# Attention and two feed-forward layers on one core: an earlier cut of d_ff for tiles 0 and 1, and a planner that runs forward and backward

## The chip, the cores and the metric

The kernel runs on one core of a Trainium2 chip. Its engines work side by side: TensorE (PE, with its weight loads as PEld), VectorE (DVE), ScalarE (ACT), GpSimd (POOL) and SyncE (SP), whose queue issues every DMA here. The metric is the device time of one execution in microseconds (us), the median over runs; less is better. Before the change it is 654.42 us (three runs, 654.26 to 655.8).

## The reference

What is computed, with the heads folded back into rows between attention and the first layer:

```python
scores = q @ k.T / 8                       # batch 2, 8 heads, 768 positions, head size 64
keep = (pos_k < n_sink) | (0 <= pos_q - pos_k < window)      # n_sink 4, window 128
a = exp(where(keep, scores, -1e9) - max);  a = a / (sum(a) + 1e-9)
x = (a @ v)                                # 1536 rows x 512
h = x @ w1_in;  g = max(h, 0) + alpha * min(h, 0);  x = g @ w1_out      # d_ff 2048
h = x @ w2_in;  g = max(h, 0) + log1p(exp(-abs(h)));  out = g @ w2_out  # d_ff 2048
```

## The kernel before

The 1536 rows are four tiles of 384 (t = 0 to 3). Attention of a tile is six groups, G = 6t to 6t+5; a group is 128 queries of two head pairs. `front` computes a group's scores on TensorE (L470, 24 matmuls), reduces and masks them on DVE (L475, four of them), exponentiates on ACT (L478, four) and scales (L492, on DVE, ACT or POOL); `back` turns them (L504 and L505, eight transposes), copies them out of PSUM (L160 or L156, two of 128x512), multiplies by the values (L523, 24 matmuls), and leaves x as a rounded half and a rest (L164, `x<-bank,x`, on DVE).

Each layer cuts d_ff = 2048 into 16 slices c. One (t, c) is a place p in a list. `g1` multiplies x by the slice of the first weights (12 matmuls, L274), an activation follows (`act1`: ACT L290 and L291, DVE L292, then two halves g by L156/L158/L160 and L164; `act2` in layer 2: ACT L309, L310, L312 and DVE L307, L313, L314, L164), and the second product is `g2` (12 matmuls, L327, in layer 1) or `g2_out` (9 matmuls, L368, in layer 2). The `h` of successive places lies in banks 4 and 5 by turns. A weight slice comes as 64-bit numbers and has to be converted first (`convert`): one load (SP) and, of about 1000 columns each, DVE L248, L250, L252, an ACT or POOL step (L239/L241), DVE L255, an ACT or POOL copy (L156/L158), DVE L164 (`w<-temp,w`). A slice is usable by TensorE only behind this last subtraction. Slices 0 to 15 of layer 1 are converted once, in order.

The order of layer 1 before: tiles 0 and 1 with slices 0 to 7, tile 0's eight first; then both with slices 8 to 15; then tiles 2 and 3 in the same way. The sums of `g2` collect in banks 0 to 3 over a run of slices and are then kept or added in SBUF (`keep_y`, L339 and L344). The attention of tile 1 is spread between the first slices of tile 0 and uses one bank pair (6, 7) throughout, as every later tile does; tile 0 has four pairs.

What sets the order on every engine is `Planned.run`: it holds all operations with a cost by engine, what they read and write, and a due time from the table `slots` (L565). It walks once through time and gives each free engine the ready operation with the earliest due time; an operation with a choice of engines goes where it would end first. The operations are then emitted in the order of their planned starts, so each engine's queue is in that order, and an instruction whose operand is late holds up all behind it on its engine. At run time nothing is reordered.

Two constraints matter at the step from layer 1 to layer 2: `act2` of odd places writes into the part of `late` that holds tile 3's kept sum, so it waits until the four L344 of tile 3 have read it; and `g1` of place p+2 waits until L314 of place p has read its bank.

Of the kernel before, what the change touches and what calls it, by code (L numbers as in the profile page):

```python
# [8 lines left out]
F32 = mybir.dt.float32  # L9
# [38 lines left out]
class Planned:  # L48
# [6 lines left out]
    TO_PE, FROM_PE, BETWEEN, FROM_DMA = 0.23, 0.20, 0.15, 2.2  # L55

# [28 lines left out]
    def run(self):  # L85
        ops = self.ops
        left = [len(o[2]) for o in ops]
        after = [[] for _ in ops]
        for n, o in enumerate(ops):
            for b in o[2]:  # L90
                after[b].append(n)
        engines = ("SP", "PE", "ACT", "DVE", "POOL")
        free = dict.fromkeys(engines, 0.0)
        waiting = {e: [] for e in engines}
        ready = {e: [] for e in engines}
# [8 lines left out]

        for n in range(len(ops)):
            if not left[n]:
                offer(n)
        def queue(e, n):
            due = ops[n][3] + 30
            return 1.8 * sum(ops[m][1][e] for d, m in ready[e] if m not in start and m != n and d <= due and len(ops[m][1]) == 1)  # L110

        t, force = 0.0, False
        while len(start) < len(ops):
            for e in engines:
                while waiting[e] and waiting[e][0][0] <= t + 1e-9:
                    n = heapq.heappop(waiting[e])[1]
                    if n not in start:
                        heapq.heappush(ready[e], (ops[n][3], n))
            for e in engines:
# [3 lines left out]
                while ready[e]:  # L123
                    due, n = heapq.heappop(ready[e])
                    if n in start:
                        continue
                    cost = ops[n][1]
                    mine = t + cost[e]
                    if not force and any(max(free[o], at(n, o)) + c + queue(o, n) < mine + queue(e, n) - 1e-9 for o, c in cost.items() if o != e):
                        later.append((due, n))  # L130
                        continue
                    start[n], end[n], on[n] = t, mine, e
                    free[e] = mine
                    for m in after[n]:
# [6 lines left out]
            nxt = [free[e] for e in engines if free[e] > t + 1e-9]  # L141
            nxt += [waiting[e][0][0] for e in engines if waiting[e] and waiting[e][0][0] > t + 1e-9]
            if len(start) < len(ops):
                force = not nxt
                t = min(nxt, default=t)
        for n in sorted(start, key=lambda n: (start[n], n)):
            ops[n][0](self.nc, on[n])
# [19 lines left out]
class Memory:  # L167
# [4 lines left out]
    def __init__(self, tc, ctx):  # L172
# [6 lines left out]
        self.temp = temp = pool.tile([128, 3 * 1024], F32, name="temp")  # L179
# [7 lines left out]
        self.ring = [(late[:, n * RB:(n + 1) * RB], ("ring", n)) for n in range(3)]  # L187
# [12 lines left out]
        self.z = [temp[:, 2048 + n * 512:2560 + n * 512].bitcast(BF16) for n in range(2)]  # L200
# [13 lines left out]
class Ffn:  # L214
# [7 lines left out]
    def convert(self, l, c, n, due, load):  # L222
# [20 lines left out]
        def first(nc, e):  # L243
# [5 lines left out]
            {"DVE": 0.69}, [hi, lo], [kz], due)  # L249
# [150 lines left out]
class Window:  # L400
# [15 lines left out]
    def ring(self, G, c):  # L416

        if G == 0 or G >= 12:
            n = (2 * G + c) % 3 if G else c
# [4 lines left out]
    def load(self, G, c, due):  # L424
        t, b, j, _, hp = self.where(G)
        buf, k = self.ring(G, c)

        def go(nc, e):
            if 0 < G < 12 and c == 0:
                self.kept[15 - G % 6] = self.mem.slot(f"w{15 - G % 6}", [128, 2 * RB], F32)  # L430
            nc.sync.dma_start(out=buf(), in_=self.kqv[b, j, hp + c])

        keys = [k] + ([("kqv", 15 - G % 6, 1)] if 0 < G < 12 and c == 0 else [])
        if 12 <= G < 14:
            keys += self.mem.under[(2 * G + c) % 3]
# [8 lines left out]
    def front(self, G, d0, d1):  # L444
# [6 lines left out]
        for c in range(2):  # L451
            buf, kr = self.ring(G, c)

            def scores(nc, e, c=c, buf=buf):
                ring = buf()
# [15 lines left out]
            add(scores, {"PE": 0.52}, [kr], kb, d0)  # L471
# [362 lines left out]
```

## Time and profile before

| | us |
|---|---|
| median of 3 runs | 654.42 |
| the profiled execution | 653.59 |
| its span, first to last instruction | 651.8 |
| busy in the span: PE, PEld | 627.3, 575.2 |
| busy in the span: DVE, ACT, POOL | 481.1, 315.2, 81.6 |

The execution's time is 1.8 us over its span. A busy PE is not a PE at its peak: matmuls are pipelined and the end of one lies past the start of the next, so how fast PE works is read from the distance between starts. The page's 40 slices have DVE at 8 or 9 tenths in nearly all of the first nine and PE at 5 to 8 tenths in the first three. From 390 us to 640 us PE is busy without a break.

### The profile page before, as it was taken

Reading aid. Unit: us, or ns where it says so; the run is one execution under the profiler, and the core shown is the slowest. Engines: PE = TensorE matmul, PEld = TensorE weight load, DVE = VectorE, ACT = ScalarE, POOL = GpSimd, SP = SyncE. Lnnn points to the kernel's source line nnn. Section 1 sums busy time; section 2 is a strip of 40 time slices with the busy share of each in tenths; the row PEclk is TensorE's granted clock in tenths of the full one; section 3 lists DMA queues with packets and bytes.
Section 4 is the critical chain, followed back from the end, with each engine's and each line's share of the span. In section 5 each row is a group of like instructions: output and inputs, shape, how many; then the busy total and the mean of one; then the engine's idle time right before and its main releaser. Section 6 shows DMA issues by size and latency. Waiting matters only on the chain.

```text
span 651.8 us, 10937 instructions
## 1 busy us (share of the span) xinstructions
PE 627.3 (96%) x4224; PEld 575.2 (88%) x4224; DVE 481.1 (74%) x1064; ACT 315.2 (48%) x707; POOL 81.6 (13%) x103
## 2 busy tenths in 40 slices
PE   5888999999999999999999989999999999999995
PEld 4677889999999999999999989999999999999994
DVE  5899999884454654469887988886787777677674
ACT  3776766663334543435643645553443433333332
POOL 1445423430000100002310201000000000000000
PEclk9999999999999999999999989999999999999999
DMA  7999350111211112056105630000010000000001
GB/s 270 350 363 398 129 208 2 52 52 55 96 54 52 51 51 73 5 202 251 64 1 182 213 123 1 0 1 2 1 41 9 33 17 1 0 25 25 2 1 53
DMA packets 15035, 57.14 MB, mean 88 GB/s; under 512 B 1920, under 2 KB 4480, under 8 KB 14976
## 3 DMA queue, kind: packets, MB, share of 16 engines
q1 hardware_dynamic: 14976, 56.37, 24.1%
q8 instruction: 35, 0.57, 0.4%
q14 instruction: 24, 0.20, 0.1%
HBM read 53.22 MB, written 3.15 MB: 86 GB/s over the span
## 4 chain that ended last, share of the span: by engine, by line
PE 81%; DVE 11%; DMA 3%; POOL 2%; issue 1%; ACT 0%; SPq 0%; POOLq 0%; DVEq 0%
PE bank L274 36%; PE bank L368 20%; PE bank L327 17%; PE bank L470 3%; PE bank L523 2%; DVE w L164 1%; DVE temp L255 1%; PE bank L504 1%; DVE g L164 1%; DVE temp L252 1%; PE bank L505 1%; DVE temp L248 1%; DVE r L292 1%; DMA w<-w 1%; DMA w<-kqv 1%
## 5 line engine op out<-in xcount | busy, mean ns | idle before, releaser
L274 PE MATMUL bank<-x,w 128*128 128x384 f32 x1536 | 297.1, 339 | 4.0 <-DVE late L314 2.1
L274 PEld LDWEIGHTS bank<-x,w 128*128 128x128 f32 x1536 | 271.0, 189 | 12.9 <-DVE late L314 2.6
L327 PE MATMUL bank<-g,w 128*128 128x384 f32 x768 | 154.2, 341 | 2.2 <-ACT g L156 1.9
L368 PE MATMUL bank<-w,g 128*128 128x512 f32 x576 | 143.1, 393 | 0.0
L327 PEld LDWEIGHTS bank<-g,w 128*128 128x128 f32 x768 | 132.2, 188 | 6.8 <-ACT g L156 2.4
L368 PEld LDWEIGHTS bank<-w,g 128*128 128x128 f32 x576 | 107.2, 188 | 19.6
L309 ACT ACTIVATE late<-bank 128x384 f32<-128x384 f32 x64 | 31.3, 491 | 120.6 <-PE bank L274 120.6
L290 ACT ACTIVATE r<-bank 128x384 f32<-128x384 f32 x64 | 31.3, 490 | 76.5 <-PE bank L274 71.0
L292 DVE SCALAR_TENSOR_TENSOR r<-r,alpha,r 128x384 f32<-128x384 f32 x64 | 41.0, 640 | 27.2 <-ACT r L291 27.1
L307 DVE TENSOR_SCALAR late<-late 128x384 f32<-128x384 f32 x64 | 23.8, 373 | 45.1 <-ACT late L310 45.0
L312 ACT ACTIVATE late<-late 128x384 f32<-128x384 f32 x64 | 33.5, 525 | 24.8 <-DVE late L307 24.7
L478 ACT ACTIVATE late<-late,st 128x224 f32<-128x224 f32 x72 | 33.8, 471 | 22.0 <-DVE st L475 22.0
L164 DVE TENSOR_TENSOR w<-temp,w 128x1024 fp32r<-128x1024 f32 x32 | 38.8, 1219 | 5.1 <-ACT w L156 2.9
L492 POOL TENSOR_SCALAR late<-late,st 128x224 f32<-128x224 f32 x33 | 25.0, 768 | 130.6 <-DVE st L483 89.6
L164 DVE TENSOR_TENSOR g<-r,g 128x384 fp32r<-128x384 f32 x64 | 37.2, 581 | 5.3 <-POOL g L158 4.1
L255 DVE SCALAR_TENSOR_TENSOR temp<-w,temp 128x1024 int32<-128x1024 int32 x32 | 40.0, 1250 | 0.9 <-ACT temp L239 0.7
L164 DVE TENSOR_TENSOR g<-late,g 128x384 fp32r<-128x384 f32 x64 | 35.5, 557 | 5.3 <-POOL g L158 0.4
L475 DVE CUSTOM_DVE_ANT_0 late<-bank,mask 128x224 f32<-128x224 f32 x72 | 24.2, 386 | 19.9 <-PE bank L470 19.7
L164 DVE TENSOR_TENSOR late<-late 128x384 f32<-128x384 f32 x64 | 35.5, 556 | 1.8
L313 DVE SCALAR_TENSOR_TENSOR late<-late 128x384 f32<-128x384 f32 x64 | 35.5, 556 | 1.6
L314 DVE SCALAR_TENSOR_TENSOR late<-bank,late 128x384 f32<-128x384 f32 x64 | 35.5, 556 | 0.0
L310 ACT ACTIVATE late<-late 128x384 f32<-128x384 f32 x64 | 33.4, 524 | 1.7
(87 smaller groups left out, 591.4 us busy)
## 6 DMA issues: line engine op xcount, KB each, us to landing
w<-w SPq DMA_DIRECT2D x32, 1023.8 KB, 5.2
late<-kqv SPq DMA_DIRECT2D x26, 400.0 KB, 3.7
w<-kqv SPq DMA_DIRECT2D x22, 400.0 KB, 6.5
out<-late SPq DMA_DIRECT2D x18, 128.0 KB, 1.7
out<-early SPq DMA_DIRECT2D x2, 256.0 KB, 2.7
out<-early SPq DMA_DIRECT2D x2, 128.0 KB, 2.5
raw<-nsw SPq DMA_DIRECT2D x1, 2.0 KB, 3.1
alpha<-alpha SPq DMA_DIRECT2D x1, 8.0 KB, 4.1
```

Source lines behind the costliest of these rows:

```text
L164: engine(nc, e).tensor_tensor(out, a, b, ALU.subtract)
L255: add(lambda nc, e: nc.vector.scalar_tensor_tensor(b, raw[0].rearrange("p n w -> p (n w)").bitcast(I32)[:, 0:2048:2], 13, b, ALU.logical_s ...
L274: nc.tensor.matmul(out=h, lhsT=w[:, a, kk], rhs=xt[:, b, kk], start=(kk == 0 and n == 0), stop=(kk == 3 and n == 2))
L290: add(lambda nc, e: nc.scalar.activation(r, h, AF.Relu), {"ACT": 0.485}, [kh], [("r", 0)], due)
L292: add(lambda nc, e: nc.vector.scalar_tensor_tensor(n, n, mem.alpha[:, c:c + 1], r, ALU.mult, ALU.add), {"DVE": 0.61}, [("r", 0), ("alpha", ...
L310: add(lambda nc, e: nc.scalar.activation(u, u, AF.Exp, scale=-1.0), {"ACT": 0.53}, [], [ku], due)
L312: add(lambda nc, e: nc.scalar.activation(l, w, AF.Ln), {"ACT": 0.53}, [kw], [kl], due)
L313: add(lambda nc, e: nc.vector.scalar_tensor_tensor(u, w, 1.0, u, ALU.subtract, ALU.subtract), {"DVE": 0.57}, [kw], [ku], due)
L314: add(lambda nc, e: nc.vector.scalar_tensor_tensor(l, h, 0.0, l, ALU.max, ALU.add), {"DVE": 0.56}, [kh], [kl], due)
L327: nc.tensor.matmul(out=self.mem.bank[m][:, 0:TT], lhsT=w[:, a, m], rhs=g[:, b], start=(ends[0] and part == 0 and n == 0), stop=(ends[1] an ...
L368: nc.tensor.matmul(out=self.mem.bank[bk], lhsT=g[:, a, m * 128:(m + 1) * 128], rhs=w[:, b], start=(c == 0 and part == 0 and n == 0), stop= ...
L478: add(lambda nc, e, u=u: nc.scalar.activation(s[:, u], s[:, u], AF.Exp, bias=st[:, 0, u:u + 1], scale=-1.0, accum_out=st[:, 1, u:u + 1]), ...
```

## The change

Five edits.

1. The list of layer 1 is cut at slice 4 for tiles 0 and 1 (`cuts`): tile 0 with slices 0 to 3, tile 1 with 0 to 3, tile 0 with 4 to 15, tile 1 with 4 to 15. Tiles 2 and 3 stay cut at 8. `keep_y` and the first and last flags of `g2` follow the cut.
2. Groups 6 to 9 of tile 1 get the four bank pairs in turn (`place`), as tile 0 has; groups 10 and 11 stay on banks 6 and 7. Their due times are closer (`30 + 4 * r`).
3. Scores of a group are one operation of 24 matmuls, where they were two of 12, and its two loads are one operation.
4. The ring for the loads of groups 16 to 23 has a fourth buffer, `spare`, which also holds the second 16-bit scratch of `convert`.
5. `run` plans nine times. `forward` is the old walk with due times given; `backward` walks from the end over the engines that the forward plan chose, and gives each operation an urgency, the latest moment at which it may end. Eight times the urgencies of the last plan become the due times of the next. The plan that ends first by its own costs is emitted.

```diff
-    def run(self):
+    def forward(self, due):
 ...
-                        heapq.heappush(ready[e], (ops[n][3], n))
+                        heapq.heappush(ready[e], (due[n], n))
 ...
+    def backward(self, end, on):
+        left = [len(a) for a in self.after]
+        done = {}
+        for n in range(len(ops)):
+            if not left[n]:
+                waiting[on[n]].append((0.0, n))
 ...
+                    free[e] = done[n] = t + ops[n][1][e]
+                    for m in ops[n][2]:
+                        left[m] -= 1
+                        if not left[m]:
+                            wanted = max(done[k] + self.lag(on[m], on[k]) for k in self.after[m])
+                            heapq.heappush(waiting[on[m]], (wanted, m))
 ...
+        last = max(done.values())
+        return [last - done[n] for n in range(len(ops))]
+
+    def run(self):
 ...
+        plans = [self.forward([o[3] for o in self.ops])]
+        for _ in range(self.AGAIN):
+            plans.append(self.forward(self.backward(*plans[-1][2:])))
+        last, start, end, on = min(plans, key=lambda p: p[0])
 ...
-            n = (2 * G + c) % 3 if G else c
+            n = (2 * G + c) % (3 if G < 16 else 4) if G else c
 ...
-        n0 = (0, 2, 4, 6)[G % 4] if G < 6 else 6
+        n0 = (0, 2, 4, 6)[G % 4] if G < 10 else 6
 ...
-            add(scores, {"PE": 0.52}, [kr], kb, d0)
+        add(scores, {"PE": 1.02}, list(kr), kb, d0)
 ...
-    layer1 = [(t0 + t, c0 + c) for t0 in (0, 2) for c0 in (0, 8) for t in range(2) for c in range(8)]
+    cuts = ((0, 4, 16), (0, 8, 16))
+    layer1 = [(2 * n + t, c, a, b) for n in range(2) for a, b in zip(cuts[n], cuts[n][1:]) for t in range(2) for c in range(a, b)]
-    slots = 8 * [6.8] + 32 * [5.3] + 88 * [4.2]
+    slots = 4 * [8.0] + 4 * [5.0] + 32 * [5.3] + 88 * [4.2]
```

Where it moves instructions, first on PE in the opening. In the names, `x0` and `x1` are the inputs of tiles 0 and 1, `w0` to `w15` the weight slices, L274 is `g1` and L327 `g2`. Before, at tile 1's first product:

```order
L327 MATMUL bank3_64<-g0_153,w6_922 128x384 x2
L327 MATMUL bank0_61<-g0_153,w6_922 128x384
L327 MATMUL bank1_62<-g0_153,w6_922 128x384
L327 MATMUL bank2_63<-g0_153,w6_922 128x384
L327 MATMUL bank3_64<-g0_153,w6_922 128x384
L274 MATMUL bank5_66<-x0_150,w7_1024 128x384 x6
L274 MATMUL bank4_65<-x1_151,w0_456 128x384 x12
```

The same place of the changed program (L318 is `g1`, L371 `g2`):

```order
L371 MATMUL bank0_61<-g0_154,w3_850 128x384
L371 MATMUL bank3_64<-g0_154,w3_850 128x384
L318 MATMUL bank5_66<-x1_152,w1_618 128x384 x3
L371 MATMUL bank1_62<-g0_154,w3_850 128x384 x2
L318 MATMUL bank4_65<-x1_152,w0_507 128x384 x6
L371 MATMUL bank2_63<-g0_154,w3_850 128x384 x2
L371 MATMUL bank1_62<-g0_154,w3_850 128x384
L371 MATMUL bank2_63<-g0_154,w3_850 128x384
L318 MATMUL bank5_66<-x1_152,w1_618 128x384 x6
L318 MATMUL bank4_65<-x1_152,w2_747 128x384 x12
```

Tile 1's products stood behind eight slices of tile 0; now they stand behind four, and work of both tiles is interleaved in pieces of a quarter or half of a slice.

On DVE, up to the last subtraction of weight slice 14 of layer 1, before (`st` and `mask` belong to attention, `r1` and `g` to the activation, `x2` to tile 2):

```order
L250 TENSOR_SCALAR temp_73<-temp_73 128x1024
L252 TENSOR_TENSOR temp_73<-temp_73 128x1024
L292 SCALAR_TENSOR_TENSOR r1_70<-r1_70,alpha_74,r0_69 128x384
L255 SCALAR_TENSOR_TENSOR temp_73<-w14_796,temp_73 128x1024
L164 TENSOR_TENSOR x2_152<-bank6_67,x2_152 128x2x128
L164 TENSOR_TENSOR g0_153<-r1_70,g0_153 128x384
L255 SCALAR_TENSOR_TENSOR temp_73<-w15_832,temp_73 128x1024
L164 TENSOR_TENSOR w14_1517<-temp_73,w14_1517 128x1024
```

and of the changed program (L207 is that L164, L299 is L255, L336 is L292, L294 and L296 are L250 and L252):

```order
L336 SCALAR_TENSOR_TENSOR r1_70<-r1_70,alpha_75,r0_69 128x384
L299 SCALAR_TENSOR_TENSOR temp_73<-w14_1062,temp_73 128x1024
L294 TENSOR_SCALAR temp_73<-spare_74 128x1024
L207 TENSOR_TENSOR g1_155<-r1_70,g1_155 128x384
L296 TENSOR_TENSOR spare_74<-spare_74,temp_73 128x1024
L207 TENSOR_TENSOR w14_1582<-temp_73,w14_1582 128x1024
```

The subtraction of slice 14 stands at nearly the same place of DVE's list, with slice 15 one step less far, and what was done of the activations ahead of it is one place more.

Last, PE at the step from layer 1 to layer 2, where `x1` is layer 2's first input and L368 is `g2_out`. Before:

```order
L274 MATMUL bank5_66<-x1_151,w1_2964 128x384 x12
L327 MATMUL bank0_61<-g0_153,w15_1544 128x384 x2
L327 MATMUL bank1_62<-g0_153,w15_1544 128x384 x2
L327 MATMUL bank2_63<-g0_153,w15_1544 128x384 x2
L327 MATMUL bank3_64<-g0_153,w15_1544 128x384 x2
L327 MATMUL bank0_61<-g0_153,w15_1544 128x384
L327 MATMUL bank1_62<-g0_153,w15_1544 128x384
L327 MATMUL bank2_63<-g0_153,w15_1544 128x384
L327 MATMUL bank3_64<-g0_153,w15_1544 128x384
L274 MATMUL bank4_65<-x1_151,w2_3006 128x384 x12
L368 MATMUL bank0_61<-w0_2904,g0_153 128x512 x2
```

and of the changed program (L412 is `g2_out`):

```order
L318 MATMUL bank5_66<-x1_152,w1_2964 128x384 x3
L371 MATMUL bank1_62<-g0_154,w15_1628 128x384 x2
L371 MATMUL bank0_61<-g0_154,w15_1628 128x384
L371 MATMUL bank1_62<-g0_154,w15_1628 128x384
L371 MATMUL bank2_63<-g0_154,w15_1628 128x384 x3
L371 MATMUL bank3_64<-g0_154,w15_1628 128x384 x3
L318 MATMUL bank5_66<-x1_152,w1_2964 128x384 x9
L318 MATMUL bank4_65<-x1_152,w2_2982 128x384 x12
L412 MATMUL bank0_61<-w0_2890,g0_154 128x512 x2
```

Nine of the twelve products of slice 1 moved from ahead of the last `g2` of tile 3 to behind it.

## Rows read from the trace of the kernel before

**Rows 1.** Stretches: busy us of each engine (instructions), granted clock, DMA.
```profile
core 0: us, PE busy (x) PEld busy (x) DVE busy (x) ACT busy (x) POOL busy (x), PEclk, DMA share, GB/s
20.00:40.00 20.00, 16.44 (x245) 12.58 (x242) 17.41 (x54) 14.29 (x39) 8.72 (x14) 1.00 0.91 358
40.00:60.00 20.00, 18.15 (x193) 16.24 (x190) 19.02 (x45) 14.51 (x37) 12.12 (x12) 1.00 0.95 380
60.00:92.40 32.40, 30.86 (x285) 26.94 (x284) 31.61 (x68) 23.23 (x57) 10.00 (x10) 1.00 0.47 170
380.00:390.00 10.00, 7.86 (x31) 6.84 (x30) 8.60 (x16) 5.49 (x12) 1.09 (x1) 0.83 0.18 75
```

**Rows 2.** Timeline of PE, 63 to 71 us: start, duration, what, count.
```profile
63.65 0.27 PE L504 MATMUL bank<-ident,late 128*128 128x128 f32 x1
...
64.44 2.34 PE L274 MATMUL bank<-x,w 128*128 128x384 f32 x12
66.71 1.12 PE L523 MATMUL bank<-late,w 96*64 96x128 f32 x24
67.76 0.79 PE L274 MATMUL bank<-x,w 128*128 128x384 f32 x3
...
70.09 1.00 PE L470 MATMUL bank<-w 64*64 64x224 f32 x24
```

**Rows 3.** Chain of waits near 100 us: start, us, what.
```profile
100.89 2.08 PE bank L327 x12
```

**Rows 4.** Timeline of DVE: the last subtractions of weight slices 8 and 14.
```profile
91.36 1.22 DVE L164 TENSOR_TENSOR w<-temp,w 128x1024 fp32r<-128x1024 f32 x1
...
136.94 1.22 DVE L164 TENSOR_TENSOR w<-temp,w 128x1024 fp32r<-128x1024 f32 x1
```

**Rows 5.** Timeline of PE at the same time.
```profile
138.02 0.61 PE L470 MATMUL bank<-late 64*64 64x224 f32 x12
```

**Rows 6.** Groups of DVE: busy us, mean ns, then idle before and releasers.
```profile
L292 DVE SCALAR_TENSOR_TENSOR r<-r,alpha,r 128x384 f32<-128x384 f32 x64 | 41.0, 640 | 27.2 <-ACT r L291 27.1
L255 DVE SCALAR_TENSOR_TENSOR temp<-w,temp 128x1024 int32<-128x1024 int32 x32 | 40.0, 1250 | 0.9 <-ACT temp L239 0.7
...
L164 DVE TENSOR_TENSOR g<-r,g 128x384 fp32r<-128x384 f32 x64 | 37.2, 581 | 5.3 <-POOL g L158 4.1 <-ACT g L156 0.3
...
L475 DVE CUSTOM_DVE_ANT_0 late<-bank,mask 128x224 f32<-128x224 f32 x72 | 24.2, 386 | 19.9 <-PE bank L470 19.7
```

**Rows 7.** Groups of ACT: an exponential, a 128x512 copy, the accumulator.
```profile
L478 ACT ACTIVATE late<-late,st 128x224 f32<-128x224 f32 x72 | 33.8, 471 | 22.0 <-DVE st L475 22.0
...
L156 ACT ACTIVATE late<-bank 128x512 f32<-128x512 f32 x31 | 17.5, 596 | 16.5 <-PE bank L505 16.3
L478 ACT ACTIVATION_READ_ACCUMULATOR late<-late,st 128x1 f32 x72 | 13.5, 188 | 0.0
```

**Rows 8.** Timeline of ACT: second step of the activation of the third product.
```profile
55.43 0.48 ACT L291 ACTIVATE r<-bank 128x384 f32<-128x384 f32 x1
```

**Rows 9.** Timeline of PE near 150 us: a group's second half of scores.
```profile
150.60 1.75 PE L274 MATMUL bank<-x,w 128*128 128x384 f32 x9
152.27 0.61 PE L470 MATMUL bank<-late 64*64 64x224 f32 x12
152.82 0.79 PE L274 MATMUL bank<-x,w 128*128 128x384 f32 x3
```

**Rows 10.** Timeline of all engines, 375 to 388 us: the step between the layers.
```profile
375.37 2.24 PE L327 MATMUL bank<-g,w 128*128 128x384 f32 x12
...
378.20 1.48 DVE L344 TENSOR_TENSOR early<-bank,late 128x384 f32<-128x384 f32 x3
...
379.53 2.25 PE L368 MATMUL bank<-w,g 128*128 128x512 f32 x9
...
379.73 0.87 ACT L309 ACTIVATE late<-bank 128x384 f32<-128x384 f32 x2 [2.25 <-PE bank L274]
...
383.32 1.01 DVE L314 SCALAR_TENSOR_TENSOR late<-bank,late 128x384 f32<-128x384 f32 x2
383.92 3.91 PE L274 MATMUL bank<-x,w 128*128 128x384 f32 x12 [2.14 <-DVE late L314]
```

More of the change, by code (lines that the diff above doesn't have):

```diff
@@ L55 @@
     TO_PE, FROM_PE, BETWEEN, FROM_DMA = 0.23, 0.20, 0.15, 2.2
+    ENGINES, AGAIN = ("SP", "PE", "ACT", "DVE", "POOL"), 8
     def __init__(self, nc):
@@ L83, in lag @@
         return self.FROM_PE if a == "PE" else self.BETWEEN
-    def run(self):
+    def forward(self, due):
         ops = self.ops
         left = [len(o[2]) for o in ops]
[L88 to L95, printed above, removed]
+        free = dict.fromkeys(self.ENGINES, 0.0)
+        waiting = {e: [] for e in self.ENGINES}
+        ready = {e: [] for e in self.ENGINES}
         end, on, start = {}, {}, {}
@@ L103, in offer, with queue, elsewhere @@
                 heapq.heappush(waiting[e], (at(n, e), n))
+        def queue(e, n):
+            return 1.8 * sum(ops[m][1][e] for d, m in ready[e]
+                             if m not in start and m != n and d <= due[n] + 30 and len(ops[m][1]) == 1)
+        def elsewhere(n, e, t):
+            mine = t + ops[n][1][e] + queue(e, n) - 1e-9
+            return any(max(t, free[o], at(n, o)) + c + queue(o, n) < mine for o, c in ops[n][1].items() if o != e)
         for n in range(len(ops)):
@@ L107, in run @@
                 offer(n)
-        def queue(e, n):
-            due = ops[n][3] + 30
-            return 1.8 * sum(ops[m][1][e] for d, m in ready[e] if m not in start and m != n and d <= due and len(ops[m][1]) == 1)
         t, force = 0.0, False
         while len(start) < len(ops):
-            for e in engines:
+            for e in self.ENGINES:
                 while waiting[e] and waiting[e][0][0] <= t + 1e-9:
@@ L123, in run @@
                 while ready[e]:
-                    due, n = heapq.heappop(ready[e])
+                    d, n = heapq.heappop(ready[e])
                     if n in start:
                         continue
[L127 to L130, printed above, removed]
+                    if not force and elsewhere(n, e, t):
+                        later.append((d, n))
                         continue
-                    start[n], end[n], on[n] = t, mine, e
-                    free[e] = mine
-                    for m in after[n]:
+                    start[n], end[n], on[n] = t, t + ops[n][1][e], e
+                    free[e] = end[n]
+                    for m in self.after[n]:
                         left[m] -= 1
@@ L140, in run @@
                     heapq.heappush(ready[e], x)
-            nxt = [free[e] for e in engines if free[e] > t + 1e-9]
-            nxt += [waiting[e][0][0] for e in engines if waiting[e] and waiting[e][0][0] > t + 1e-9]
+            nxt = [free[e] for e in self.ENGINES if free[e] > t + 1e-9]
+            nxt += [waiting[e][0][0] for e in self.ENGINES if waiting[e] and waiting[e][0][0] > t + 1e-9]
             if len(start) < len(ops):
@@ L450, in front, with scores @@
         mask = mem.mask[:, min(j, 2)]
[L451 to L455, printed above, removed]
+        bufs, kr = zip(*(self.ring(G, c) for c in range(2)))
+        def scores(nc, e):
+            for c in range(2):
+                ring = bufs[c]()
                 for part in range(2):
@@ L738 @@
         first = Window(mem, InOrder(nc), kqv)
-        first.load(0, 0, 0)
-        first.load(0, 1, 0)
+        first.load(0, 0)
         nc.sync.dma_start(out=mem.alpha, in_=alpha)
```

70 lines of the change are left out of this document (44 added, 26 removed).

## The prediction

> **What bounds the kernel now.** I read first the busy time by stretches [rows 1]. From 20 to 92 us DVE has no room: 17.4 of 20 us, 19.0 of 20, 31.6 of 32.4, while PE is busy for 16.4, 18.2 and 30.9 of the same. The DMA engines stand at 0.91 and 0.95 up to 60 us, but there is no load among what TensorE waits for; it waits for conversions and copies, which are DVE's and ACT's. From 390 to 640 us PE is busy without a break.
>
> Busy time hides how much PE loses, so I read its timeline by starts. Twelve matmuls of a slice take 2.08 us [rows 3]; a group's transposes 0.79 (63.65 to 64.44), its values 1.05 (66.71 to 67.76), its scores 0.93 (the 1.00 less the overlap of 0.07 that the values show) [rows 2]. These are the prices of undisturbed work. The twelve `g1` matmuls between two pieces of attention take 2.27 instead of 2.08 (64.44 to 66.71) [rows 2], so an interruption costs about 0.2 us.
>
> Now a balance. Slice 14's last subtraction ends at 136.94 + 1.22 = 138.16 [rows 4]. PE is then at the last half of a group's scores [rows 5], with 17 `g1`, 15.7 `g2`, 14.5 scores, 14 transposes and 14 values done: 32.7 x 2.08 + 14.5 x 0.93 + 14 x 0.79 + 14 x 1.05 = 107.2 us of work. It has lost 31 us. The whole change is about how many of these 31 come back, since afterwards PE works nearly without gaps to the end, and what PE gains there the end gains too. PE's instructions are the same in number in both programs.
>
> **The change part by part.**
>
> *The opening.* DVE paces it, so I count DVE's list ahead of slice 14's last subtraction in both orders. Changed against before, it holds one L292 (0.64), one L164 of `g` (0.58) and four L475 (0.39 each) more, and less one L255 (1.25) [rows 6] and two 128x512 copies, which go to ACT (0.60 each by ACT's price [rows 7]); casts and small steps both ways cancel. 0.64 + 0.58 + 1.56 - 1.25 - 1.20 = 0.3 us more: the same list. So slice 14 comes again at about 138. But PE has more to do ahead of its first use: in the new order `g1` of slice 14 is the 19th product (14 of tile 0 and four of tile 1 stand ahead; before, the 23rd). Ahead of it stand 18 `g1`, 17 `g2`, 15 scores, 15 transposes and 14 values: 35 x 2.08 + 15 x 0.93 + 15 x 0.79 + 14 x 1.05 = 113.3 us. If DVE keeps its pace and PE is then waiting at slice 14, PE stands 113.3 - 107.2 = 6.1 us further at the same moment. That is the gain if all goes well; DVE could also idle less than before, because two tiles give PE and ACT something to do sooner, so I put the upper end at -8.
>
> Against it stands ACT. All of tile 1's attention now comes ahead of slice 3. Up to the second step of the third product ACT's list before is reached at 55.43 + 0.48 = 55.9 [rows 8]. The fourth product of tile 0 in the new order has twelve more exponentials ahead of it (0.471 + 0.188 = 0.66 each) and eight more 128x512 copies (0.60) [rows 7]: 7.9 + 4.8 = 12.7 us, and with small steps (one activation step pair of 0.97 [rows 8] and some copies of x, less one conversion step) 14.5. ACT was at work for about 0.89 of the time (42.4 us of listed work since 8 us), so these take 16 us: ACT reaches that step at about 72, where DVE's list alone would put it near 67. In the worst case the 5.5 us are never regained and the gain is about 0; if they are, because eleven more slices follow in which ACT has room (23.2 of 32.4 us [rows 1]), it is 6.1. Value: -4, which leaves ACT a third of the gain. Ends: -8 and 0.
>
> *Whole scores instead of halves.* After 92 us, scores of eleven of the twelve groups 12 to 23 were cut in two by other matmuls; in the new order none is. The cut costs: a half goes from 152.27 to 152.82, 0.55, so two are 1.10 against 0.93, and the nine matmuls in front take 1.67 (150.60 to 152.27) against 9 x 2.08 / 12 = 1.56 [rows 9]. That is 0.2 to 0.28 a group. The pieces of attention between products fall from 47 to 39; 8 x 0.25 = -2.0. Ends: 0 (if the free time goes to the next wait) and -3.5 (0.28 for eleven groups and a few bubbles behind the split).
>
> *The step between the layers.* Before, the last `g2` of tile 3 starts at 375.37 and ends near 377.3. The four L344 follow it, to 378.20 + 1.48 = 379.68; L309 of place 1 may only write then and starts at 379.73; its chain (L309 to L314) ends at 383.32 + 1.01 = 384.3 with the second half, and PE waits 2.14 us for the first [rows 10]. The chain from the last `g2` to L314 is some 6.6 us; what PE had in hand was `g1` of slice 2 (2.08) and a first `g2_out` (2.05), 4.1 us, before `g1` of slice 3 needs the bank. Now nine of twelve matmuls of slice 1's `g1` (1.56) stand behind the last `g2`, so 5.7 us are in hand against a chain of about 6.7: the wait falls by 1.1 to about 1.0.
>
> Behind the wait of before the twelve matmuls take 3.91 us, where those at 375.37 take 2.24 [rows 10]: 1.67 lost. The granted clock of these 10 us is 0.83 [rows 1], a mix of the full 2.4 GHz and its half, and the half follows directly on the 2.14 us wait. In the opening, PE waits about 10 to 20 per cent of 40 us in small pieces, with the granted clock at 1.00 [rows 1]; a wait of 1.0 us is of that sort, so I expect 1.00 here and the 1.67 saved. The Trainium skill says the same of cause and effect, in "TensorE: Matmul & The Clock Gate", Part 1: The HAM clock gate: the array's clock is gated to half when PE has been idle, and activity gives it back; by that rule alone a shorter gap that still falls badly would keep its half clock, and the step would bring 1.1 instead of 2.7. Value: -1.1 - 1.6 = -2.7, taken as -2.5. Ends: 0 (nine matmuls only shift the wait) and -3.1 (the wait vanishes wholly).
>
> *The rest.* Loads: a group's two become one operation with both DMAs, and a fourth buffer frees the ring; no load is among what PE waits for, so 0. From the last matmul to the end nothing moves in kind; 0. The plan sets each instruction as late as its own costs allow, so a step that takes longer on the chip than in the plan has less slack, on all engines at once. The trace of before shows no such plan; below, 0; above, 4: twenty waits of 0.2 us, what an interruption costs [rows 2]. Value: +1, a quarter, since PE's list is long and steady after 390 us.
>
> *Sum.* -4 - 2 - 2.5 + 1 = -7.5 on the profiled execution's 653.59: 646.1. The median of before is 0.83 above its profiled execution, so the median of after should be 646.1 + 0.83 = **647.0**.
>
> **The rivals.**
>
> *ACT becomes the bound of the opening.* For it: the 72 against 67 above. Against it: 0.89 is a rate under waits, not a limit, and some copies may go to POOL, busy for 8.7 of 20 us [rows 1]. If the whole 5.5 us stay, the opening gives 0.6 instead of 4: 650.4, say 651. Chance 0.18.
>
> *Half clock in the opening.* Now `g1` of slice 1 for tile 1 stands in PE's list ahead of attention pieces of group 7, and slices 0 and 1 end about 6.7 us of DVE work apart with 2.08 us of products between: a wait of up to 4.5 us, longer than the one after which the clock halved. For it: the row at 383.92 [rows 10]. Against it: the clock stayed at 1.00 through all of the opening before [rows 1]. It costs up to 1.67 us [rows 10]: 648.5. Chance 0.15.
>
> *The opening's gain is eaten up and the boundary wait stays.* Only the whole scores count, against the tight plan: -2 + 1 = -1, 653. Chance 0.08.
>
> *Slower: fresh slices.* Slices 4 to 15 now come in a row for tile 0 alone, each needed as soon as it is converted, where before eight products of tile 1 gave DVE time to get ahead. DVE's new list from slice 7 to slice 14 holds 44.7 us of work, counted as above. Before, from slice 8 (91.36 + 1.22 = 92.58) to slice 14 (138.16) it took 45.6 us for 38.3 of listed work [rows 4], 1.19 for 1. If waits on ACT and POOL raise this, slice 14 is late. The gain in all, 6.1 here and 4.5 for scores and step less the 1, is 9.6; it is used up when slice 14 comes at 138.2 + 9.6 = 147.8, that is from 1.19 + 9.6 / 44.7 = 1.40 for 1 on. At 1.47 it comes 2.9 us later still, and the time is 654.42 + 2.9, about 657. For it: PE cannot fill such waits, as tile 1's rest stands behind tile 0's slices. Against it: DVE is already at 0.98 in that stretch [rows 1]. Chance 0.09.
>
> *The change does not do what it says:* excluded; the changed order shows tile 1 behind four slices and the nine matmuls behind the last `g2`.
>
> **How the numbers follow.** Forecast 647.0 with 0.50; the rivals 0.18, 0.15, 0.08, 0.09. The likeliest has -4 +- 2, -2 +- 1, -2.5 +- 1 and +1 +- 1.5: about 643 to 650.5. Below it stand -8 - 3.5 - 3.1 = -14.6 at the extreme; I go to 640.5, near the middle between that (639.8 with the median) and the forecast's own end. Above, 653.5 takes in the rivals of ACT, of the clock and most of the third; the last and the tails are left out. A change of 0.3% (1.96 us) is about what a measurement of this kernel can tell from none: faster is under 652.46, slower over 656.4. Faster: 0.47 of the forecast's 0.50, 0.14 of the clock's 0.15, 0.14 of ACT's 0.18, 0.03 of the third's 0.08: 0.78. Slower: 0.07 of the last rival, 0.04 of the tails of ACT and the third: 0.11. Within: 0.11.
>
> **What would show it.** Opening: tile 1's first product on PE between 68 and 75 us, slice 14's last subtraction within 3 us of 138, and PE's loss at that moment near 25 where it was 31. If ACT shows no idle time from 10 to 65 us and DVE's waits end on ACT, the rival of ACT holds; a granted clock under 1.00 before 90 us is that of the clock; slice 14 later than 146 us is the slower one. Scores: each in one piece of about 1.00 us from 92 us on. Step: a wait of at most 1.2 us for L314 and a granted clock of 1.00 around 380 us; a longer wait with 0.83 makes that term wrong. If from 390 us to the end PE has gaps that sum to over 2 us, the tight plan costs more than I gave it.

## The result and the profile after

The changed kernel takes 640.03 us (median of four runs, 639.41 to 641.09) against 654.34 for the kernel before in the same runs; the ratio is 0.978, 95% interval 0.9767 to 0.9794. The change gave 14.3 us where 7.4 were forecast, and the time lies half a microsecond under the low end of the range, 640.5. The profiled execution took 641.09 us, the longest of the four, with a span of 639.1; between the two profiled executions the difference is 12.5 us, and the account below is of these.

The balance of the prediction (time passed less PE's work at undisturbed prices) can be taken at any moment from the starts of the matmuls. So many us PE had lost by then:

| | by 40 us | 92.4 | 143 | 366 | 390 | 620 |
|---|---|---|---|---|---|---|
| before | 21.0 | 29.0 | 31.0 | 40.6 | 44.5 | 45.8 |
| after | 16.9 | 21.0 | 23.8 | 29.6 | 31.6 | 33.0 |

So the opening up to 143 us gave 7.2 us, the attention between products from 143 to 366 us 3.8, the step between the layers 1.9, and the rest -0.1: 12.8 in all, which is the difference of the spans (12.7).

The stretches after, which answer to [rows 1] (columns as there):

```profile
20.00:40.00 20.00, 17.91 (x303) 14.25 (x300) 19.71 (x77) 18.32 (x61) 14.90 (x23) 1.00 0.98 368
40.00:60.00 20.00, 19.69 (x204) 17.14 (x202) 17.73 (x46) 14.77 (x43) 15.12 (x17) 1.00 0.85 350
60.00:92.40 32.40, 31.76 (x238) 30.54 (x236) 31.39 (x53) 20.76 (x41) 10.84 (x10) 1.00 0.60 233
366.00:380.00 14.00, 12.27 (x64) 10.97 (x63) 13.39 (x26) 8.53 (x16) 2.76 (x2) 1.00 0.29 112
```

All three engines that feed PE are fuller from 20 to 40 us than before (DVE 19.7, ACT 18.3, POOL 14.9), and PE with them. The granted clock is 1.00 in each stretch, at the step between the layers too, which now lies between 366 and 380 us.

Slice 14's last subtraction, from DVE's timeline [rows 4], and PE at that time [rows 5]:

```profile
135.21 1.93 DVE L207 TENSOR_TENSOR w<-temp,w 128x1024 fp32r<-128x1024 f32 x1 [0.28 <-ACT w L199]
```

```profile
134.65 2.53 PE L371 MATMUL bank<-g,w 128*128 128x384 f32 x13
137.02 0.68 PE L318 MATMUL bank<-x,w 128*128 128x384 f32 x3
137.63 1.12 PE L568 MATMUL bank<-late 96*64 96x128 f32 x24
```

Slice 14 is ready at 137.1 (forecast 138), and PE takes up its first product (137.02, three matmuls) just then. By 138 us PE has done 114.2 us of work; 113.3 were reckoned ahead of that product, 107.2 were done before.

A group's scores are one piece from 92 us on, here from PE's timeline near 107 us; they answer to [rows 9]:

```profile
106.33 0.51 PE L371 MATMUL bank<-g,w 128*128 128x384 f32 x2
106.77 1.00 PE L514 MATMUL bank<-late 64*64 64x224 f32 x24
107.70 2.70 PE L371 MATMUL bank<-g,w 128*128 128x384 f32 x14
```

106.77 to 107.70 is 0.93, the undisturbed price. Last the step between the layers on PE, against [rows 10]:

```profile
365.10 3.80 PE L318 MATMUL bank<-x,w 128*128 128x384 f32 x21
368.74 2.25 PE L412 MATMUL bank<-w,g 128*128 128x512 f32 x9
372.71 2.35 PE L318 MATMUL bank<-x,w 128*128 128x384 f32 x12 [1.73 <-DVE late L358]
374.90 1.08 PE L412 MATMUL bank<-w,g 128*128 128x512 f32 x4
```

The wait fell from 2.14 to 1.73 us only, but the matmuls behind it take 2.35 us instead of 3.91.

### The profile page after: what moved, and what is told of

Its sections match the earlier page's. It is cut to its first block, busy times and chain, and to the rows that moved or that the text cites. A ratio compares the mean times of both kernels' runs of the same rounds, so it can differ in the third digit from the quotient of the medians.

```text
span 639.1 us, 10922 instructions
## 1 busy us (share of the span) xinstructions
PE 619.0 (97%) x4224; PEld 574.1 (90%) x4224; DVE 479.0 (75%) x1061; ACT 313.9 (49%) x704; POOL 82.8 (13%) x109
## 4 chain that ended last, share of the span: by engine, by line
PE 86%; DVE 7%; POOL 3%; ACT 2%; issue 1%; DMA 0%; DVEq 0%; POOLq 0%; ACTq 0%
PE bank L318 39%; PE bank L412 20%; PE bank L371 18%; PE bank L568 3%; PE bank L514 2%; POOL late L537 2%; PE bank L549 1%; DVE temp L299 1%; PE bank L550 1%; DVE late L520 1%; DVE r L336 1%; DVE g L207 1%; POOL g L201 1%; DMA raw<-nsw 0%; DVE early L520 0%
## 5 line engine op out<-in xcount | busy, mean ns | idle before, releaser
L318 PE MATMUL bank<-x,w 128*128 128x384 f32 x1536 | 293.3, 337 | 1.7 <-DVE late L358 1.7
L318 PEld LDWEIGHTS bank<-x,w 128*128 128x128 f32 x1536 | 269.9, 188 | 8.4 <-DVE late L358 2.2
L371 PE MATMUL bank<-g,w 128*128 128x384 f32 x768 | 152.4, 339 | 0.3 <-DVE g L207 0.2
L412 PE MATMUL bank<-w,g 128*128 128x512 f32 x576 | 143.0, 393 | 0.0
L371 PEld LDWEIGHTS bank<-g,w 128*128 128x128 f32 x768 | 132.8, 188 | 2.7 <-DVE g L207 0.5
L412 PEld LDWEIGHTS bank<-w,g 128*128 128x128 f32 x576 | 107.2, 188 | 19.5
L334 ACT ACTIVATE r<-bank 128x384 f32<-128x384 f32 x64 | 31.4, 490 | 76.2 <-PE bank L318 71.6
L336 DVE SCALAR_TENSOR_TENSOR r<-r,alpha,r 128x384 f32<-128x384 f32 x64 | 42.3, 661 | 25.7 <-ACT r L335 25.5
L351 DVE TENSOR_SCALAR late<-late 128x384 f32<-128x384 f32 x64 | 23.3, 364 | 40.3 <-ACT late L354 40.3
L356 ACT ACTIVATE late<-late 128x384 f32<-128x384 f32 x64 | 33.5, 524 | 23.7 <-DVE late L351 23.6
L207 DVE TENSOR_TENSOR w<-temp,w 128x1024 fp32r<-128x1024 f32 x32 | 41.4, 1294 | 2.0 <-POOL w L201 1.0
L207 DVE TENSOR_TENSOR g<-late,g 128x384 fp32r<-128x384 f32 x64 | 35.5, 555 | 9.6 <-ACT g L199 4.0
L299 DVE SCALAR_TENSOR_TENSOR temp<-w,temp 128x1024 int32<-128x1024 int32 x32 | 41.3, 1297 | 0.9 <-ACT temp L283 0.8
L537 POOL TENSOR_SCALAR late<-late,st 128x224 f32<-128x224 f32 x34 | 26.3, 785 | 107.9 <-DVE st L528 65.9
L207 DVE TENSOR_TENSOR g<-r,g 128x384 fp32r<-128x384 f32 x64 | 35.9, 561 | 4.1 <-POOL g L201 3.2
L207 DVE TENSOR_TENSOR late<-late 128x384 f32<-128x384 f32 x64 | 35.6, 556 | 1.6
L335 ACT ACTIVATE r<-bank 128x384 f32<-128x384 f32 x64 | 31.1, 486 | 9.8 <-DVE g L207 9.8
L358 DVE SCALAR_TENSOR_TENSOR late<-bank,late 128x384 f32<-128x384 f32 x64 | 35.5, 555 | 0.5 <-ACT late L356 0.5
```

What stands on the lines that cost most here:

```text
L207: engine(nc, e).tensor_tensor(out, a, b, ALU.subtract)
L299: add(lambda nc, e: nc.vector.scalar_tensor_tensor(b, raw[0].rearrange("p n w -> p (n w)").bitcast(I32)[:, 0:2048:2], 13, b, ALU.logical_s ...
L318: nc.tensor.matmul(out=h, lhsT=w[:, a, kk], rhs=xt[:, b, kk], start=(kk == 0 and n == 0), stop=(kk == 3 and n == 2))
L336: add(lambda nc, e: nc.vector.scalar_tensor_tensor(n, n, mem.alpha[:, c:c + 1], r, ALU.mult, ALU.add), {"DVE": 0.61}, [("r", 0), ("alpha", ...
L356: add(lambda nc, e: nc.scalar.activation(l, w, AF.Ln), {"ACT": 0.53}, [kw], [kl], due)
L358: add(lambda nc, e: nc.vector.scalar_tensor_tensor(l, h, 0.0, l, ALU.max, ALU.add), {"DVE": 0.56}, [kh], [kl], due)
```

## The experiments

All were timed beside the kernel before, whose median was between 653.76 and 655.00 us. A ratio and its 95% interval are estimated from the single runs and need not equal the quotient of the medians. Lost time is PE's, reckoned as in the table above, and is that of the one profiled execution.

**One part of the prediction at a time, in the kernel before.** The plan's order is kept, and single instructions are moved in it. `before_whole` joins the halves of the scores of groups 12 to 23 on PE alone:

```diff
+        halves = [n for n, o in enumerate(ops) if o[0].__name__ == "scores"]
+        for one, two in zip(halves[24::2], halves[25::2]):
+            order.remove(one)
+            order.insert(order.index(two), one)
```

> The kernel before in its own order, but from group 12 on the first half of a group's scores is moved behind, next to the second; no other engine's order changes. The term of the prediction: twelve halves joined at 0.25 us, some 2 us less: 651.5 to 652.5. Theory of the trace after (3.7 us between 143 and 366 us come from whole scores): 650 to 651. Theory that the pieces go at nothing, since the later first half delays DVE: 654 to 655.

Measured 648.94, ratio 0.9932 (0.9908 to 0.9956). The loss from 143 to 366 us fell from 9.6 to 6.3: 3.3 us, or 0.37 for each of the nine groups whose scores stood there in two pieces before. The term is real and larger than the prediction put it. The median is 4.8 under that of before; the interval of the ratio reaches from 2.9 to 6.0 us.

`before_step` moves the nine matmuls:

```diff
+        at = max(order.index(n) for n in last)     # the last g2 of layer 1
+        for n in late:                             # three of four parts of g1, slice 1
+            order.remove(n)
+        order[at - len(late) + 1:at - len(late) + 1] = late
```

> The kernel before in its own order, but nine of the twelve matmuls of slice 1's first product in layer 2 are moved behind the last g2 of layer 1; no other engine's order changes. The term of the prediction: the wait for L314 falls from 2.14 by 1.1 us and the matmuls behind it stay at the full clock (2.2 instead of 3.9 us): 651.7. Rival (the chain behind the last g2 starts later by as much): 654 to 655, the wait at 2 us and the clock at 0.83 as before.

Measured 652.28, ratio 0.9982 (0.9970 to 0.9994). From its timeline:

```profile
376.68 3.80 PE L280 MATMUL bank<-x,w 128*128 128x384 f32 x21
380.32 2.25 PE L374 MATMUL bank<-w,g 128*128 128x512 f32 x9
384.06 2.35 PE L280 MATMUL bank<-x,w 128*128 128x384 f32 x12 [1.50 <-DVE late L320]
```

and from ACT's:

```profile
380.52 0.87 ACT L315 ACTIVATE late<-bank 128x384 f32<-128x384 f32 x2 [3.81 <-PE bank L280]
```

The wait fell by 0.6 and not 1.1; the clock stayed full. The nine matmuls that PE now has in hand are also what the chain begins with: L315 (L309 before) waits for slice 1's product and starts at 380.52, where it started at 379.73 [rows 10]. So a part of the expected rival is there too. The loss from 366 to 390 us fell from 3.9 to 1.8. The medians differ by 1.5, the ratio stands for 0.4 to 2.0. This profiled run had lost 0.9 more by 143 us than that of before, in an order that was not changed there.

**The parts of the change.** First each undone in the changed kernel; the plan is made anew each time. `plan_once` sets AGAIN to 0; `cut_at_8` restores the cut and its slots; `one_pair` has `G < 6` in `place`; `half_scores` gives the planner two operations of scores:

```diff
-    ENGINES, AGAIN = ("SP", "PE", "ACT", "DVE", "POOL"), 8
+    ENGINES, AGAIN = ("SP", "PE", "ACT", "DVE", "POOL"), 0      # plan_once
-    cuts = ((0, 4, 16), (0, 8, 16))
+    cuts = ((0, 8, 16), (0, 8, 16))                             # cut_at_8
-        n0 = (0, 2, 4, 6)[G % 4] if G < 10 else 6
+        n0 = (0, 2, 4, 6)[G % 4] if G < 6 else 6                # one_pair
-        add(scores, {"PE": 1.02}, list(kr), kb, d0)
+            add(scores, {"PE": 0.52}, [kr[c0]], kb, d0)         # half_scores, c0 = 0, 1
```

> The changed kernel (640.0 us), but planned once forward, without the eight repetitions; cut, bank pairs, whole scores and ring stay. Theory 1 (the cut makes the gain of the opening, whole scores that of the attention behind it, the planner little): 640 to 643, PE's lost time at 143 us stays near 24 us. Theory 2 (the urgencies found from the end make most of the gain): 647 or more, and the lost time at 143 us near 29.

> The changed kernel with tiles 0 and 1 cut at slice 8 again and the slots of before. Theory 1 (the cut makes the gain of the opening, since more of PE's work lies ahead of slice 14): 646 to 648, lost time at 143 us back to 29 to 31 us. Theory 2 (planner) and theory 3 (the four bank pairs): 640 to 642, lost time at 143 us near 25.

> The changed kernel with groups 6 to 9 on banks 6 and 7 again. Theory 1 (the cut): 641 to 642. Theory 3 (the four bank pairs let attention of tile 1 run ahead, which is the 4 us that PE had gained by 40 us): 644 or more, with lost time of 20 us or more at 40 us where the changed kernel has 16.9.

> The changed kernel with a group's scores as two operations of 12 matmuls for the planner, the loads still merged. Theory 1 (whole scores are what saved 3.7 us between 143 and 366 us): 642 to 644, and the halves are apart again from 92 us on. Theory 2 (the planner): 640 to 641, since the urgencies keep the halves of a group together.

And `planner_alone`: the kernel before with `forward`, `backward` and the new `run`, nothing else.

> The kernel before (654.4 us) with nothing but the new planner: cut at 8, one bank pair for tile 1, half scores, ring of three. Theory 1 (cut and bank pairs give the planner something to use, the planner alone little): 650 to 654, lost time at 143 us 28 to 31. Theory 2 (the urgencies do it alone): 646 or less, lost time at 143 us 26 or less.

| | median us | ratio to before | lost by 40 us | by 143 | 143 to 366 | 366 to 390 |
|---|---|---|---|---|---|---|
| after | 640.03 | 0.978 (0.9767 to 0.9794) | 16.9 | 23.8 | 5.8 | 2.0 |
| plan_once | 650.16 | 0.992 (0.9891 to 0.995) | 18.8 | 30.2 | 8.8 | 3.9 |
| one_pair | 648.59 | 0.9911 (0.9893 to 0.9928) | 21.1 | 30.9 | 6.0 | 2.5 |
| cut_at_8 | 646.11 | 0.9869 (0.9851 to 0.9886) | 17.8 | 29.1 | 6.8 | 2.4 |
| half_scores | 641.54 | 0.9813 (0.9788 to 0.9837) | 17.4 | 24.3 | 5.7 | 1.9 |
| planner_alone | 646.32 | 0.9902 (0.9876 to 0.9928) | 19.8 | 27.1 | 8.3 | 0.2 |

No theory holds by itself. Cut, bank pairs and repeated plan are each worth 6 to 10 us when they are taken out last, together far more than the whole change. The planner alone makes about half of the change: 7.4 us by the medians, 6.4 by the ratio. It takes 3.9 off the opening's loss, 1.3 off that up to 366 us, and 3.7 off the step, where the changed kernel itself loses 2.0. Cut and pairs pay only together. By 143 us 27.1 us are lost with the planner and neither of them (with half scores and three buffers); 30.9 with the cut alone, 29.1 with the pairs alone, and 23.8 with both. Both without the repetition come to 30.2, 0.8 under before.

Two limits. The profiles of `plan_once`, `cut_at_8` and `one_pair` hold 3.4 to 6.8 us of half clock between 32 and 45 us, those of after and `planner_alone` none from 20 us on; how much of their loss is the clock's was not separated. And the profiled run of `plan_once` took 651.97 us, near the upper end of its eight runs (645.89 to 652.16), so its row is a dear one.

Whole scores as an operation are worth 1.5 us by the medians, within the scatter of `half_scores` (639.83 to 643.59). Its eleven groups behind 92 us have their scores in one piece all the same. That is not the urgencies' doing in general: in `planner_alone` five of twelve groups are still cut. The fourth buffer and the closer due times were not tried by themselves.

**What paces the opening.** Four kernels in the changed kernel's own order. Ten instructions more on one engine:

```diff
+        more = [15.0 + 5 * k for k in range(10)]
+            if more and start[n] >= more[0] and on[n] == "ACT":      # "DVE" in more_dve
+                more.pop(0)
+                self.nc.scalar.activation(self.junk, self.junk, AF.Copy)
```

> The changed kernel in its own order, with ten more ACT instructions of some 0.45 us (128x320 copies that nobody reads), one every 5 us of the plan from 15 to 60 us. Theory that ACT bounds the opening: 4 us or more slower, 643.5 to 644.5. Theory that DVE paces it and ACT follows with room: under 1.5 us slower, 640 to 641.5, slice 14 still ready near 137 us.

> The changed kernel in its own order, with ten more DVE instructions of some 0.47 us (128x320 subtractions that nobody reads), one every 5 us of the plan from 15 to 60 us. Theory that DVE paces the opening and ACT only half: 4 us or more slower, 644 to 645, slice 14 at 141 us instead of 137. Theory that ACT and DVE share the pace, each hiding half of what the other is given: 2 to 3 us slower, 642 to 643, as with ten more ACT instructions (643.0).

and less work on one, which the output then leaves out:

```diff
+            w = 128 if 3 <= G < 12 and e == "ACT" else 512           # less_act
+            copy(nc, e, a[h][0][:, 0:w], bank[h][:, 0:w])
+        few = 256 if l == 0 and c < 4 else 1024                      # less_dve, columns of L299
```

> The changed kernel in its own order; ACT's 17 copies of turned weights of groups 3 to 11 take 128 of the 512 columns only (the output leaves the rest out): about 0.33 us less each, 5.5 in all. Theory that ACT and DVE set the pace by turns, so that an instruction on either costs 0.6 of its length: 3 us faster, 636.5 to 637.5, and slice 14 ready near 134.5. Theory that DVE alone paces and ACT only could not take more: 639 to 640. Theory that ACT bounds: 635.

> The changed kernel in its own order; L299 of slices 0 to 3 of layer 1 takes 256 of the 1024 columns only (the output leaves the low bits of these weights out): about 0.9 us less each, 3.7 in all. Theory that ACT and DVE set the pace by turns: 2 us faster, 637.5 to 638.5. Theory that DVE alone paces: 3.5 us faster, 636 to 637, slice 14 ready near 133.5. Theory that ACT bounds: 639.5 to 640.5.

| | median us | ratio to before | lost by 143 us | slice 14 ready |
|---|---|---|---|---|
| after | 640.03 | 0.978 | 23.8 | 137.1 |
| more_act | 642.96 | 0.9847 (0.9823 to 0.987) | 26.2 | 139.5 |
| more_dve | 643.06 | 0.9817 (0.9791 to 0.9842) | 27.3 | 140.6 |
| less_act | 639.85 | 0.9772 (0.9756 to 0.9789) | 24.1 | 137.5 |
| less_dve | 638.38 | 0.9749 (0.9731 to 0.9766) | 21.8 | 134.9 |

5.5 us less on ACT (17 copies, by their durations) bring nothing. Of 3.3 us less on DVE (four L299; 3.7 were reckoned) 2.0 come through by 143 us, and slice 14 comes 2.2 us sooner. Slice 14's last subtraction on DVE's timeline, of less_act and then of less_dve:

```profile
135.60 1.93 DVE L207 TENSOR_TENSOR w<-temp,w 128x1024 fp32r<-128x1024 f32 x1 [0.28 <-ACT w L199]
```

```profile
132.99 1.93 DVE L207 TENSOR_TENSOR w<-temp,w 128x1024 fp32r<-128x1024 f32 x1 [0.28 <-ACT w L199]
```

Only less and more together tell this: by more_act alone ACT would have seemed as much of a bound as DVE. How more_act costs its 2.4 us is seen on PE, on DVE, and in the stretch between (columns as in [rows 1]):

```profile
33.79 1.68 PE L573 MATMUL bank<-late,w 96*64 96x128 f32 x24 [1.66 <-ACT late L203]
```

```profile
38.06 0.39 DVE L525 CUSTOM_DVE_ANT_0 late<-bank,mask 128x224 f32<-128x224 f32 x1 [1.51 <-PE bank L519]
```

```profile
34.20:37.60 3.40, 3.40 (x44) 2.92 (x43) 2.31 (x4) 2.37 (x8) 3.17 (x3) 0.50 1.00 405
```

An added instruction at 32.3 stands ahead of the copy that PE waits for; PE then works at half clock from 34.2 to 37.6 us, and DVE waits 1.51 us for scores that are made meanwhile. Up to 34 us DVE was 0.9 us behind the changed kernel, at 38 us 2.9, and 2.4 at slice 14. So most of the cost arises at that half clock; what ten instructions on ACT would cost at full clock is not shown. In more_dve the clock stays full.

In all four traces everything is already 0.3 to 0.5 us behind the changed kernel at 18 us, ahead of the first instruction that differs. That is scatter and not the edit: in less_act DVE stays 0.4 us behind from there to 140 us, so the work taken off ACT moved nothing.

The theory of a pace set by turns, which I held after the runs with more work, falls with less_act. That DVE alone paces fits less_act, but not wholly less_dve: slice 14 at 133.5 and 636 to 637 us were expected of it, 134.9 and 638.38 measured. What held back the rest of the 3.3 us stays open.

**The plan's room.** `slack` plans with 0.1 us more for every step between engines, `slack_late` only from place 40 on, so that the opening's order stays.

```diff
-    TO_PE, FROM_PE, BETWEEN, FROM_DMA = 0.23, 0.20, 0.15, 2.2
+    TO_PE, FROM_PE, BETWEEN, FROM_DMA = 0.33, 0.30, 0.25, 2.2        # slack
+    def lag(self, a, b, n=0):                                        # slack_late
+        return self.lag0(a, b) + (0.1 if n > self.late and a != b else 0.0)
```

> The changed kernel planned with 0.1 us more for every step from one engine to another. Theory that the tight plan costs waits of 0.2 to 0.5 us on the chip (term of +1): 638.5 to 639.5. Theory that the plan's lags are right: 640 to 642.

> The changed kernel, planned with 0.1 us more for every step from one engine to another from place 40 on; the opening's order stays. Theory that the tight plan costs its room at the step between the layers (2 us lost from 366 to 390 us, 0.5 where all steps had 0.1 more): 638 to 639. Theory that the rest of that plan pays for it elsewhere: 640 to 641.

`slack`, whose order differs in the opening too, took 641.57 (0.9787): 0.4 us lost from 366 to 390 us instead of 2.0, but 27.5 by 143 us instead of 23.8. `slack_late` took 638.21 (637.87 to 639.03), ratio 0.9751 (0.9735 to 0.9768), the fastest of all: the loss by 143 us stays at 23.3, and at the step 0.3 us are lost. From its timeline, where the wait is gone:

```profile
364.11 3.80 PE L321 MATMUL bank<-x,w 128*128 128x384 f32 x21
367.75 2.25 PE L415 MATMUL bank<-w,g 128*128 128x512 f32 x9
369.83 2.34 PE L321 MATMUL bank<-x,w 128*128 128x384 f32 x12
```

**Two that gave nothing.** `step_first` moves a single L299 behind L358 at the step, `cut_4_8` cuts tiles 0 and 1 at 4 and at 8 (`cuts = ((0, 4, 8, 16), (0, 8, 16))`).

> The changed kernel in its own order but for one DVE instruction: at the step between the layers one L299 (a weight conversion, 1.78 us) stood ahead of L358 of place 1 and now stands behind it. If that instruction is what L358 is late by, the wait of 1.73 us on PE falls to about 0.6: 639 us. If the ACT step before it is (L356), nothing changes: 640.

> The changed kernel with tiles 0 and 1 cut at slices 4 and 8, so that tile 1 has eight products ahead of slice 8. Theory that fresh slices 4 to 15 in a row on tile 0 cost nothing (slice 14 comes in time for PE): 640 to 642, one more kept sum. Theory that PE still waits for slices between 4 and 8 us after slice 8: 637 to 639.

`step_first` took 640.28 (0.9779): the wait for L358 fell to 0.44 us, as expected, but a wait of 0.69 for a half of `g` stands 3 us later in its place, and from 366 to 390 us 1.7 us are lost instead of 2.0. `cut_4_8` took 642.49 (0.9818). Its profiled run, the fastest of four, has a granted clock of 0.94 from 20 to 40 us, behind waits of PE of 3.10 and 0.70 us for POOL; how much of the difference is the clock's and how much the cut's stays open.

## Why the prediction was wrong

The direction and the places were right. Two gains were put too small, the opening (4 for 7.2) and the whole scores (2 for 3.8), and the tight plan's cost too large (1 for 0.1); the step's gain was put too large (2.5 for 1.9). The four measured terms sum to 12.8 in place of 7.5. By the prediction's own sum 653.59 - 12.8 + 0.83 would be 641.6, within the range. That the time fell below it is also chance: the execution of before that was profiled lies 0.75 under its median, that of after 1.06 over.

**The opening, -4, measured -7.2.** The step that failed is the one on ACT: "Value: -4, which leaves ACT a third of the gain". The account by DVE's list held: 6.1 us if slice 14 comes at 138; it came at 137.1, and PE's work at 138 us was 7.0 us more than before. The 2 us taken off for ACT were not lost. The price was wrong: 0.471 + 0.188 = 0.66 for an exponential and 0.60 for a copy are durations, and on ACT they overlap. From ACT's timeline after:

```profile
27.81 0.47 ACT L523 ACTIVATE early<-early,st 128x224 f32<-128x224 f32 x1
28.18 0.19 ACT L523 ACTIVATION_READ_ACCUMULATOR early<-early,st 128x1 f32 x1
28.28 0.47 ACT L523 ACTIVATE early<-early,st 128x224 f32<-128x224 f32 x1
...
31.44 1.07 ACT L199 ACTIVATE late<-bank 128x512 f32<-128x512 f32 x2
32.40 0.48 ACT L523 ACTIVATE late<-late,st 128x224 f32<-128x224 f32 x1
```

From start to start an exponential with its accumulator takes 0.47 and a copy 0.48. I had used starts for PE and for DVE, but not for ACT. Twelve exponentials and eight copies are 9.5 us then and not 12.7, and in the kernel before ACT's durations from 8 to 56 us, 43.4 us in sum, cover only 34.3 of the 48: 0.71, and not the 0.89 of the prediction. There was idle time for what came. The fourth product's second step was done at 64.94:

```profile
64.08 0.49 ACT L334 ACTIVATE r<-bank 128x384 f32<-128x384 f32 x1 [0.46 <-PE bank L318]
64.46 0.48 ACT L335 ACTIVATE r<-bank 128x384 f32<-128x384 f32 x1
```

It waits for PE, not for ACT's own list; I had 72 by ACT and 67 by DVE. `less_act` settles it for the changed kernel: with 5.5 us less on ACT nothing comes sooner.

**Whole scores, -2, measured -3.8.** The step that failed is the price of a cut, "8 x 0.25". The count came nearly as said: the pieces of attention behind 92 us fell from 47 to 38 (39 forecast), although the values of two groups and the transposes of one are cut anew. `before_whole`, with nothing joined but scores, gives 3.3 us for nine groups between 143 and 366 us: 0.37 each, where 0.2 to 0.28 had been read at one place [rows 9]. In the changed kernel 11 pieces fewer stand in that stretch (27 for 38), 0.35 each on average.

**The step between the layers, -2.5, measured -1.9.** The clock's part came as said, 2.35 us for the twelve matmuls instead of 3.91. The reason given for it did not hold: a wait of about 1.0 us was to be of the small sort that leaves the clock full. The wait was 1.73, and in the openings of other runs half clock follows waits of 1.62 to 1.67 (below). At this place nine profiles of the changed kernel and its variants show waits of 1.71 to 1.74 and full clock each time, so it is no chance of one run; but by the prediction's reason it was luck. The wait fell by 0.4 instead of 1.1, since the account of the chain left out what else DVE and ACT do there; from DVE's timeline after:

```profile
370.41 1.78 DVE L299 SCALAR_TENSOR_TENSOR temp<-w,temp 128x1024 int32<-128x1024 int32 x1 [0.20 <-ACT temp L283]
372.11 0.54 DVE L358 SCALAR_TENSOR_TENSOR late<-bank,late 128x384 f32<-128x384 f32 x1
```

L358 stands behind a weight conversion, L299. In `step_first`, which moves it, the wait is 0.44, but the loss at the step falls by 0.3 us only. `before_step` showed a second omission: the moved matmuls are what the chain begins with.

**The tight plan, +1, measured +0.1 from 390 us on.** Where it does cost something is the step: `slack_late` takes 1.7 us off there and 1.8 off the time.

**The rivals.** ACT as the bound: no. Half clock in the opening: not in the changed kernel, whose granted clock is 1.00 from 20 us on; but it is there in the profiles of six other runs (below), so the chance was not misplaced. Fresh slices: slice 14 was early, and `cut_4_8`, which takes the row of twelve apart, is no faster. The far end of the sum was 639.8, and the range stopped at 640.5, which the prediction calls near the middle between that and 643 (the middle is 641.4).

What is not settled: of the 14.3 us between the medians the profiled executions show 12.5. The runs of one kernel differ by 0.7 to 3.8 us, in `plan_once` by 6.3. As far as the profiles show, this arises in the opening (`before_step` lost 1.0 more by 40 us in an unchanged order), and a part of it at the very start: the first matmuls take about twice their time (24 scores 1.98 us at 8.60 in after, 1.00 at 16.32), and the moment from which the clock is recorded as full differs. In seven profiles that begin in the order of after it is 14.7 to 17.1 us, and the loss by 18 us rises with it from 11.5 to 12.3.

## What to carry to other kernels

Price every engine by the distance of starts, the helpers too; a duration that overlaps the next one is no cost, and a busy share worked out from durations overstates the engine (ACT here: 0.89 for 0.71). To learn whether an engine sets the pace, take work off it: work added to an engine with room can still cost, because it delays a chain (in `more_act` by way of PE's clock). Parts of a schedule that only pay together (order of tiles, buffers, planner) are not priced one by one: in this kernel each of three was worth 6 to 10 us when taken out of 14.

## What the runs showed of the hardware

The granted clock after a wait of PE at the step between the layers: 0.83 over the stretch and 3.91 us for twelve matmuls behind a wait of 2.14 us [rows 1, 10]; 1.00 and 2.35 us behind waits of 1.73 (after) and 1.50 (`before_step`). In the opening of `one_pair` it falls where PE has nearly nothing for longer (stretches, columns as in [rows 1]):

```profile
29.00:32.00 3.00, 0.46 (x16) 0.27 (x8) 3.00 (x17) 3.00 (x13) 1.65 (x2) 1.00 0.94 327
32.00:35.00 3.00, 1.27 (x4) 0.45 (x4) 2.74 (x7) 0.97 (x4) 3.00 (x4) 0.60 0.96 393
35.00:38.00 3.00, 2.98 (x22) 2.28 (x24) 2.14 (x4) 2.52 (x6) 3.00 (x6) 0.50 1.00 415
```

PE works 0.46 of 3 us and 1.27 of the next 3, and is then at half its clock, 1.2 GHz. But the length of one wait does not tell whether the clock falls. From PE's timeline of `cut_at_8`:

```profile
41.14 3.92 PE L318 MATMUL bank<-x,w 128*128 128x384 f32 x12 [1.67 <-DVE x L207]
```

Behind 1.67 us the twelve matmuls take 3.92, as behind 2.14 in the kernel before; in `more_act` and `before_step` half clock stands in the opening behind waits of 1.66 and 1.62. Behind the 1.73 of after it stayed full. At the place of that 1.62, in the same order, PE waits 1.63 us in before and 1.61 in `before_whole`, and there the clock stayed full too. What decides between them no run here settles. The Trainium skill says of cause and effect, in "TensorE: Matmul & The Clock Gate", Part 1: The HAM clock gate: idling throttles the array and activity releases it; the rows agree in so far as each fall ahead of PE's last matmul stands behind a wait of PE.

What half clock costs depends on whether PE is what the others wait for. At the step it cost 1.6 us of twelve matmuls. In `before_step` 3.4 us of it from 59 us on are not seen in the loss by 92 us, which is 0.9 over that of before as it was by 40 us already. `plan_once`, whose profile has 0.88 from 30 to 40 us and 0.77 from 40 to 50, ran between 645.9 and 652.2 us, the widest of all.
